# Attention's weight sum replaced by accumulating DMAs, conversions moved to slots 7 to 16, the feed-forward's weight tiles allocated by name, and its first gate tile loaded in unit 26

## The chip, the cores and the metric

The kernel runs on one core of a Trainium2 chip. The metric is the device time of one execution in microseconds, as the median of several runs. TensorE (PE) multiplies, VectorE (DVE) and ScalarE (ACT) do elementwise work, GpSimd (POOL) too, and SyncE (SP), POOL and ACT issue DMAs. TensorE's granted clock is 1.2 or 2.4 GHz; in the tables 1.00 is the higher of them and 0.50 the lower.

## The reference

Three stages follow each other. Sizes: 4 batches, 8 heads, 576 tokens a batch, head size 64, model width 512, 8 experts of width 1024, a feed-forward layer of width 2048, 2304 tokens in all.

```
phi(x):  proj = x @ w_phi;  proj -= max|proj| over the row
         [exp(proj), exp(-proj)]
attention: kv = phi(k)^T @ v;  z = sum of phi(k)
           x = (phi(q) @ kv) / (phi(q) @ z + 1e-6)
experts:   e = argmax of the token's cosine logits / tau, gate = its softmax
           x = gate * (relu(x @ w1[e]) @ w2[e])
layer:     h = x @ w_in;  out = (h * sigmoid(h)) @ w_out
```

The weights w_in and w_out arrive in 64 bits and are converted on the chip.

## The kernel before

**Attention** runs over 32 heads, one iteration of a loop each. PE projects a head three iterations ahead; DVE takes the row maximum of the projection and subtracts it (`shift`, lines 385 and 386), which frees the projection's place in PSUM for the next head; PE multiplies the numerators and denominators of the current one (`numden`, line 474). ACT takes exponentials, and POOL the low parts of values that are split into a high and a low float for exact products.

**Conversion.** w_in and w_out are cut into 16 tiles each, w_in by columns and w_out by rows. `narrow` turns 128x512 numbers of 64 bits into 32 bits in four steps (one multiplication, on DVE in attention and on ACT later, then lines 201 or 204, 206 and 208 on DVE). Two neighbouring tiles of w_in make one weight `q` of the eight (NJP); its products use a scheme with seven combinations of four 128x256 blocks a0, a1 (of the even tile, with turned sign) and b0, b1 (of the odd one), kept in DRAM as `sscr[q]` with seven places. The even tile goes to places 0 and 1. For an odd tile `narrow` has a fifth step, the weight sum b0 + b1 (line 214), and `keep_weights` stores b0 in place 6, b1 in 2 and the sum in 3, 4 and 5. `add_weights(q, 0)` then adds place 0 to places 4, 5 and 6 with one accumulating DMA on POOL's queue, and `add_weights(q, 1)` adds place 1 to place 5. The first ten tiles (CA) are converted in attention, through the generator `Convert.step`, a few steps an iteration; the fifth step of an odd tile is the last before the next iteration's `shift`. Tiles 10 to 15 are converted in the expert stage.

**Experts.** 22 slots of 128 tokens. In slot s PE multiplies x by w1 in four parts (`mm1`), then the relu'd product of the slot before by w2 in four parts (`mm2`); it turns inputs with `xturn` (line 858) and hidden values with `hturn`. ACT and DVE split the weights (`split`, lines 837 and 838); SP loads them (`load1`, `load2`, line 801), only where the expert changes. POOL issues the gathers of tokens two slots ahead (`gather`, line 823), one add of `add_weights` a slot (slots 1 to 14, 17 and 18), and for the conversions a load (`cload`) and a store (`cstore`). A list `HOOKS` of places in slots gives the conversions five steps each: the first four call `cwork`, the first of which also loads the tile after next, and the fifth stores. Raw data has two buffers and the result one (`J[i]`).

**Layer.** 32 units, 8 for each of four blocks of 576 tokens: unit u multiplies weight q = u mod 8 in seven products `prod(u, n)`, in the order n = 1, 5, 4 of the unit before, 6, 3 of the unit before, 2, 7. ACT copies (`keep`, line 1083) and DVE joins (`join`, line 1090) the results; SP stores them to `hd` (line 1096). A written plan `at(unit, n, task)` hangs tasks behind products: the conversion of w_out (`oload`, `cwork`, `cstore`), and from unit 26 on `ofetch`, `ohigh`, `olow`, which load eight converted output weights of 512 KB and split them (lines 1124, 1127, 1131). The gate tile `gload(i)` reads 128 tokens of `hd` (1 MB, line 1143) and `gate` applies the activation, the high cast and the low subtraction (lines 1157 to 1159); `down` multiplies by the output weights. `gload(0)` takes a buffer of the pool `ul` that the conversions of w_out used before; `gload(1)`, `gload(2)` and later ones take buffers of pool `dr`, which is opened, on the right side of the memory, when `ur` with the tiles `wb` of weights 4 to 7 is closed. All engines' orders are as written, and DMAs of one queue are issued in that order. A tile of a later pool waits for the readers of the tiles on whose place it lies (`reuse_waits="tile"`).

```
htile(0, (0, 0))
for q in (4, 7, 6, 5):
    wspace(q)
wfetch(4)
wfetch(5)
```

Of the kernel before, what the change touches and what calls it, by code (L numbers as in the profile page):

```python
# [10 lines left out]
F32R = mybir.dt.float32r  # L11
# [3 lines left out]
ALU = mybir.AluOpType  # L15
# [4 lines left out]
P = 128  # L20
# [12 lines left out]
NJ = FF2 // P  # L33
TN = 288
NJP = NJ // 2
# [9 lines left out]
CA = 10  # L45
# [21 lines left out]
def moe_kernel(ctx, tc, qk, v, w_phi, emb, tau, w1, w2, win, wout, out):  # L67
    nc = tc.nc
# [10 lines left out]
    sscr = [dram.tile([P, 7, 256], F32, name=f"sscr{i}") for i in range(NJP)]  # L79
# [91 lines left out]
    def keep_weights(i, c, rw, dma=nc.sync):  # L171
        half, j = divmod(i, NJ)
        q, odd = divmod(j, 2)
        c = c.bitcast(F32)
        if half:
            dma.dma_start(out=woscr[q][:, odd, :], in_=c)
        elif odd:
            both = rw.rearrange("p f t -> p (f t)")[:, 0:256].bitcast(F32)
            dma.dma_start(out=sscr[q][:, 6, :], in_=c[:, 0:256])
            dma.dma_start(out=sscr[q][:, 2, :], in_=c[:, 256:512])  # L180
            dma.dma_start(out=sscr[q][:, 3:6, :], in_=both.unsqueeze(1).to_broadcast([P, 3, 256]))
        else:
            dma.dma_start(out=sscr[q][:, 0:2, :], in_=c.rearrange("p (a f) -> p a f", a=2))

    def add_weights(q, n):
        src = sscr[q][:, n:n + 1, :]
        if n:
            nc.gpsimd.dma_start(out=sscr[q][:, 5:6, :], in_=src, accum_op=ALU.add)
        else:
            nc.gpsimd.dma_start(out=sscr[q][:, 4:7, :], in_=src.to_broadcast([P, 3, 256]), accum_op=ALU.add)  # L190

    def narrow(rw, c, eng, i):
        minus = i < NJ and i % 2 == 0
        lo, hi = rw[:, :, 0], rw[:, :, 1]
        if eng is nc.scalar:
            nc.scalar.mul(out=c.bitcast(F32), in_=hi.bitcast(F32), mul=2.0 ** -112)
        else:
            eng.tensor_scalar(out=c.bitcast(F32), in0=hi.bitcast(F32), scalar1=2.0 ** -112, scalar2=None, op0=ALU.mult)
        yield
        if minus:  # L200
            nc.vector.tensor_scalar(out=lo, in0=lo, scalar1=29, scalar2=-2147483648, op0=ALU.logical_shift_right,
                                    op1=ALU.bitwise_or)
        else:
            nc.vector.tensor_scalar(out=lo, in0=lo, scalar1=29, scalar2=None, op0=ALU.logical_shift_right)
        yield
        nc.vector.scalar_tensor_tensor(out=c, in0=c, scalar=3, in1=lo, op0=ALU.logical_shift_left, op1=ALU.bitwise_or)
        yield
        nc.vector.scalar_tensor_tensor(out=c, in0=hi, scalar=-2147483648, in1=c, op0=ALU.bitwise_and,
                                       op1=ALU.bitwise_xor)
        if i < NJ and i % 2:  # L210
            yield
            a, b = c.bitcast(F32)[:, 0:256], c.bitcast(F32)[:, 256:512]
            both = rw.rearrange("p f t -> p (f t)")[:, 0:256].bitcast(F32)
            nc.vector.tensor_tensor(out=both, in0=a, in1=b, op=ALU.add)
# [32 lines left out]
    def phase_all(ctx):  # L247
# [517 lines left out]
        pools = {}  # L765
# [48 lines left out]
        def load2(s, parts=(0, 1)):  # L814
            if s < 2:
                st["e", s] = (nc.sync.value_load(regs_a[0:1, 2, POS[s]:POS[s] + 1], min_val=0, max_val=E - 1), None)
            fetch(raw2, w2, s, parts)

        def gather(s):
            xg = mp.tile([P, DM], F32, tag="t2a", name="xg", bufs=3)  # L820
            n = (B - 1) * S if s < NP else NT
            p = POS[s]
            nc.gpsimd.indirect_dma_start(out=xg, out_offset=None, in_=xd[0:n, :],
                                         in_offset=bass.IndirectOffsetOnAxis(ap=gidx[:, p:p + 1], axis=0))
            st["xg", s] = xg
# [116 lines left out]
            next(todo, None)  # L942
            keep_weights(i, c, rw, dma)

        HOOKS = [(s, n) for s in (2, 3, *range(7, 17)) for n in ((1, 5, 7) if s % 2 == 0 and s > 2 or s == 3 else (1, 5))]

        def convert(s, n):
            if (s, n) not in HOOKS:
                return
            i, n = divmod(HOOKS.index((s, n)), 5)  # L950
            if n == 0 and i and CA + i + 1 < NJ:
                cload(CA + i + 1)
            if n < 4:
                cwork(CA + i)
            else:
                cstore(CA + i, nc.gpsimd)
# [7 lines left out]

        def wspace(q):
            wb = (big.tile([P, 2, 2048], F32R, tag="blk", name="wb") if q < 4 else
                  pools["ur"].tile([P, 2, 7 * 256], F32R, tag="wb", name="wbr", bufs=4))
            W[q] = (wb[:, 0, 0:7 * 256], wb[:, 1, 0:7 * 256])

        def wfetch(q):  # L970
            if q < 4:
                wspace(q)
            nc.sync.dma_start(out=W[q][1].bitcast(F32), in_=sscr[q].rearrange("p a f -> p (a f)"))
# [77 lines left out]
        def xsplit(k, name):  # L1051
            xhigh(k, name)
            xlow(k, name)
# [215 lines left out]
        for g in range(-2, G):  # L1269
            b, h = divmod(g, H)  # L1270
# [133 lines left out]
        def route(*key):  # L1404
            if key in PLAN:
                next(more)
# [7 lines left out]
        for s in range(1, NSF + 1):  # L1414
            if s + 1 < NSF:
                load2(s + 1, (0,))
            if 1 < s < NSF:
                load2(s, (1,))
            if s == 20:
                wfetch(0)  # L1420
            if s == 21:
                wfetch(1)
                wfetch(2)
            if s < NSF:
                if s + 2 < NSF:
                    gather(s + 2)
                q, n = divmod(s - 1 if s < 15 else s - 3 if s > 16 else 99, 2)
                if q < NJP:
                    add_weights(q, n)
                for k in range(4):  # L1430
                    mm1(s, k)
                    if (s, k) == RANK:
                        ranks(B - 1, rbank)
                    route(1, s, k)
                    if s + 1 < NSF and k < 3:
                        split(s + 1, 1, k)
                    convert(s, k)
                    if k > 1 and 18 <= s < 21 and 2 * (s - 18) + k - 2 < 5:
                        xscale(0, 2 * (s - 18) + k - 2)
                    if s == NSF - 1:  # L1440
                        for f, *a in TAIL[k]:
                            f(*a)
                relu(s)
                if s + 1 < NSF:
                    xturn(s + 1)
                    split(s + 1, 1, 3)
            if 1 < s:
                ystore(s - 2)
            if s == 17:
                rp_ctx.close()  # L1450
                x_ctx.close()
                bm_ctx.close()
                sp = ctx.enter_context(tc.tile_pool(name="sp", bufs=2, **T))
                xfetch(0, 0)
                xfetch(0, 1)
            for i in range(4):
                mm2(s - 1, i)
                if s < NSF:
                    split(s, 2, i)
                else:  # L1460
                    for f, *a in TAIL[4 + i]:
                        f(*a)
                route(2, s - 1, i)
                if i == 0 and s + 3 < NSF:
                    load1(s + 3, (0,))
                if i == 0 and s + 2 < NSF:
                    load1(s + 2, (1,))
                convert(s, 4 + i)
                if i > 1 and 18 <= s < 21:
                    n = 2 * (s - 18) + i - 2  # L1470
                    if n < 5:
                        xprep(0, n)
                        if n < 3:
                            xfetch(0, n + 2)
                    else:
                        xsplit(0, "B11")
            if s < NSF:
                hturn(s)
            if s == NSF - 1:
                xfetch(1, 0)  # L1480
                xfetch(1, 1)
                wfetch(3)
            if s < NSF:
                yout(s - 1)
            if s == NSF - 1:
                for n in (1, 5, 2):
                    prod(0, n)
# [11 lines left out]
        def at(u, n, *task):  # L1499
            todo.setdefault((u, n), []).append(task)  # L1500

        htile(0, (0, 0))
        for q in (4, 7, 6, 5):
            wspace(q)
        wfetch(4)
        wfetch(5)
        def plan():
# [33 lines left out]
                at(27 + m, 6, ohigh, 2 * m + 1)  # L1541
                at(27 + m, 3, olow, 2 * m + 1)
            at(24, 7, nc.scalar.activation, vec[0:1, 0, 0:1], vec[0:1, 0, 0:1], AF.Silu)
            at(29, 1, gload, 0)
            at(30, 6, gate, 0, 0)
            at(31, 6, gate, 0, 1)

# [27 lines left out]
    with ExitStack() as c2:  # L1575
        phase_all(c2)
# [31 lines left out]
```

## Time and profile before

| | |
|---|---|
| median of three runs | 939.63 us (939.2 to 941.2) |
| the profiled execution | 941.78 us, of which the span of the trace is 940.1 us |
| busy in the span | PE 909.0, DVE 629.5, ACT 583.6, POOL 253.1 us |
| mean granted clock of PE | 0.989 |

Attention takes about the first 240 us, the experts lie up to about 530, the layer's units up to 731 and its second product up to the end. A busy engine is one that has an instruction under way; the ends of PE's instructions are modelled. Times are counted from the span's start. In rows of the timeline the first number is the start and the second the duration, or the whole stretch where several instructions are merged (x4), and the bracket holds the idle time before it and what ended it.

### The profile page before, as it was taken

To read this page: it belongs to the slowest core of one execution; us is meant where nothing else is said; L and a number is where in the kernel's file an instruction comes from. 1 tells how busy PE (TensorE), PEld (TensorE's weight loads), DVE (VectorE), ACT (ScalarE), POOL (GpSimd) and SP (SyncE) were. 2 spreads that over 40 slices of the span, in tenths; PEclk is the share of its full clock that TensorE was granted. 3 is DMA by queue.
4 is the path that set the end of the run, shared out by engine and by line. 5 is a ranking of instruction groups with operands and counts; after the bars stand their busy time and mean duration, and the time that the engine had idled before them with its cause. 6 is when DMAs were issued, how large, how long until landed. Compare 5 with 4: busy or idle time off the path is not lost. (4 is left out here: it accounts for less than half of the span.)

```text
span 940.1 us, 15670 instructions
## 1 busy us (share of the span) xinstructions
PE 909.0 (97%) x5567; PEld 791.5 (84%) x5567; DVE 629.5 (67%) x976; ACT 583.6 (62%) x948; POOL 253.1 (27%) x231
## 2 busy tenths in 40 slices
PE   8999999999999999999999899999997899999997
PEld 6999999988777778888888799999997688888885
DVE  7889898986799989989988756575763122222221
ACT  6777878745977778889888664444453233444441
POOL 6878877712212503222200020201000100010000
PEclk9999999999999999999999999999998899999999
DMA  6455353349486825993697565877694844444420
GB/s 179 115 143 171 91 177 92 102 138 355 169 218 208 257 101 177 323 305 116 218 374 267 201 202 175 253 241 244 227 311 128 202 112 112 113 112 118 118 68 22
DMA packets 135106, 170.50 MB, mean 181 GB/s; under 512 B 34696, under 2 KB 95880, under 8 KB 135024
## 3 DMA queue, kind: packets, MB, share of 16 engines
q1 hardware_dynamic: 124432, 144.84, 49.0%
q0 software_dynamic: 10512, 24.58, 9.3%
q8 instruction: 45, 0.74, 0.3%
q14 instruction: 37, 0.30, 0.1%
q10 hardware_dynamic: 80, 0.03, 0.0%
HBM read 169.43 MB, written 50.33 MB: 234 GB/s over the span
## 5 line engine op out<-in xcount | busy, mean ns | idle before, releaser
L838 DVE TENSOR_TENSOR wl<-raw,wh 128x1024 fp32r<-128x1024 f32 (+1 forms) x166 | 189.1, 1178 | 26.8 <-ACT wh L837 21.0
L837 ACT CAST wh<-raw 128x1024 fp32r<-128x1024 f32 (+1 forms) x166 | 161.4, 1025 | 24.1 <-DMA raw<-w 10.7
L1159 DVE TENSOR_TENSOR hlt<-gt,hlt 128x1024 fp32r<-128x1024 f32 x34 | 41.7, 1226 | 153.3 <-ACT hlt L1158 153.3
L788 PE MATMUL po<-wob,hlt 128*128 128x512 f32 x272 | 107.8, 396 | 3.9 <-ACT hlt L1158 3.9
L1083 ACT COPY ht<-puA 128x288 f32<-128x288 f32 x128 | 50.8, 399 | 96.4 <-PE puA L790 82.1
L790 PE MATMUL po<-wob,hlt 128*128 128x512 f32 x272 | 109.6, 403 | 0.0
L789 PE MATMUL po<-wob,hlt 128*128 128x512 f32 x272 | 108.2, 398 | 0.0
L424 POOL TENSOR_TENSOR kl<-ke,kh 128x640 fp32r<-128x640 f32 x52 | 85.2, 1657 | 31.9 <-issue 23.6
L1179 ACT COPY os<-po 128x512 f32<-128x512 f32 x17 | 10.0, 586 | 107.7 <-PE po L790 107.7
L474 PE MATMUL pnx<-kv,qp 128*128 128x73 f32 x640 | 76.6, 275 | 0.0
L474 PEld LDWEIGHTS pnx<-kv,qp 128*128 128x128 f32 x640 | 74.1, 192 | 0.1
L1180 POOL DMA_INDIRECT out<-os,oidx x18 | 17.9, 994 | 185.7 <-ACT os L1179 175.2
L788 PE MATMUL ph<-wh,xh 128*128 128x512 f32 x166 | 67.1, 404 | 0.0
L790 PE MATMUL ph<-wh,xl 128*128 128x512 f32 x166 | 65.3, 393 | 1.0 <-DVE xl L845 1.0
L788 PEld LDWEIGHTS po<-wob,hlt 128*128 128x128 f32 x272 | 51.8, 190 | 16.4 <-ACT hlt L1158 4.3
L789 PE MATMUL ph<-wl,xh 128*128 128x512 f32 x166 | 64.8, 390 | 0.0
L789 PEld LDWEIGHTS po<-wob,hlt 128*128 128x128 f32 x272 | 51.7, 190 | 13.5
L790 PEld LDWEIGHTS po<-wob,hlt 128*128 128x128 f32 x272 | 51.6, 190 | 12.6 <-DVE hlt L1159 0.8
L409 ACT ACTIVATE ke<-d 128x640 f32<-128x640 f32 x52 | 38.3, 737 | 38.1 <-DVE d L386 38.1
L385 DVE TENSOR_REDUCE m<-pqk 128x10 f32<-128x1280 f32 x32 | 47.6, 1486 | 19.1 <-PE pqk L379 19.1
L1090 DVE TENSOR_TENSOR ht<-puC,ht 128x288 f32<-128x288 f32 x64 | 29.1, 454 | 46.7 <-PE puC L790 41.8
L379 PE MATMUL pqk<-wbd,zh 128*128 128x256 f32 (+1 forms) x320 | 59.5, 285 | 0.8 <-DVE d L386 0.6
(405 smaller groups left out, 2445.8 us busy)
## 6 DMA issues: line engine op xcount, KB each, us to landing
raw<-w SPq DMA_DIRECT2D x44, 1536.0 KB
raw<-w SPq DMA_DIRECT2D x44, 512.0 KB
hd<-ht SPq DMA_DIRECT2D x124, 144.0 KB
gt<-hd SPq DMA_DIRECT2D x15, 1024.0 KB
z<-qk SPq DMA_DIRECT2D x32, 288.0 KB
wo<-wout SPq DMA_DIRECT2D x17, 512.0 KB
yd<-ys SPq DMA_DIRECT2D x23, 256.0 KB
raw<-win SPq DMA_DIRECT2D x10, 512.0 KB
```

Of the source, the lines that this page charges most:

```text
L379: nc.tensor.matmul(out=pqk[0:r, c * 256:(c + 1) * 256], lhsT=z[:, c * P:c * P + r], rhs=wbd[:, j].rearrange("p h f -> p (h f)"), start=(i ...
L385: nc.vector.tensor_reduce(out=m, in_=pv, axis=AX.X, op=ALU.max, apply_absolute_value=True)
L409: nc.scalar.activation(out=ke, in_=kd, func=AF.Exp, scale=1.0 - 2.0 * s)
L424: nc.gpsimd.tensor_tensor(out=kl[:, :, s, :], in0=st.pop(("ke", g, s)), in1=kh[:, :, s, :].bitcast(F32), op=ALU.subtract)
L474: nc.tensor.matmul(out=pn[:, c, 0:73], lhsT=qp[:, s, c * P:(c + 1) * P], rhs=kv[:, s, 0:73], start=(s == 0), stop=(s == 1))
L788: nc.tensor.matmul(out=o, lhsT=ah, rhs=bh, start=first, stop=False, skip_group_check=more)
L789: nc.tensor.matmul(out=o, lhsT=ah, rhs=bl, start=False, stop=False, skip_group_check=more)
L790: nc.tensor.matmul(out=o, lhsT=al, rhs=bh, start=False, stop=last, skip_group_check=more)
L837: nc.scalar.copy(out=hi[:, 0:n], in_=sl[:, 0:n])
L838: nc.vector.tensor_tensor(out=lo[:, 0:n], in0=sl[:, 0:n], in1=hi[:, 0:n].bitcast(F32), op=ALU.subtract)
L1083: nc.scalar.copy(out=htile(u, at), in_=BK[u, "A"])
L1159: nc.vector.tensor_tensor(out=lo, in0=g, in1=hi.bitcast(F32), op=ALU.subtract)
```

## The change

The fifth step of `narrow` is left out for tiles in attention. Their odd tiles store b0 in place 6 and b1 in places 2 to 5, and a third add, (q, 6), later adds place 6 to places 3, 4 and 5. The adds of weights 0 to 4 are thus three, those of 5 to 7 two; the list `ADDS` has 21, and slot s issues two of them from slot 8 on. `HOOKS` begins in slot 7 and has three places in each slot to 16. The tiles of weights 4 to 7 get a tag each and are allocated in rising order. `gload(0)` is called behind `prod` 4 in unit 26 instead of behind `prod` 1 in unit 29.

```diff
--- before.py
+++ after.py
@@ -174,6 +174,9 @@
         c = c.bitcast(F32)
         if half:
             dma.dma_start(out=woscr[q][:, odd, :], in_=c)
+        elif i < CA and odd:
+            dma.dma_start(out=sscr[q][:, 6, :], in_=c[:, 0:256])
+            dma.dma_start(out=sscr[q][:, 2:6, :], in_=c[:, 256:512].unsqueeze(1).to_broadcast([P, 4, 256]))
         elif odd:
             both = rw.rearrange("p f t -> p (f t)")[:, 0:256].bitcast(F32)
             dma.dma_start(out=sscr[q][:, 6, :], in_=c[:, 0:256])
@@ -182,12 +185,13 @@
         else:
             dma.dma_start(out=sscr[q][:, 0:2, :], in_=c.rearrange("p (a f) -> p a f", a=2))
 
+    ADDS = [(q, n) for q in range(NJP) for n in ((6, 0, 1) if 2 * q < CA else (0, 1))]
+
     def add_weights(q, n):
+        a, b = {6: (3, 6), 0: (4, 7), 1: (5, 6)}[n]
         src = sscr[q][:, n:n + 1, :]
-        if n:
-            nc.gpsimd.dma_start(out=sscr[q][:, 5:6, :], in_=src, accum_op=ALU.add)
-        else:
-            nc.gpsimd.dma_start(out=sscr[q][:, 4:7, :], in_=src.to_broadcast([P, 3, 256]), accum_op=ALU.add)
+        nc.gpsimd.dma_start(out=sscr[q][:, a:b, :], in_=src.to_broadcast([P, b - a, 256]) if b - a > 1 else src,
+                            accum_op=ALU.add)
 
     def narrow(rw, c, eng, i):
         minus = i < NJ and i % 2 == 0
@@ -207,7 +211,7 @@
         yield
         nc.vector.scalar_tensor_tensor(out=c, in0=hi, scalar=-2147483648, in1=c, op0=ALU.bitwise_and,
                                        op1=ALU.bitwise_xor)
-        if i < NJ and i % 2:
+        if CA <= i < NJ and i % 2:
             yield
             a, b = c.bitcast(F32)[:, 0:256], c.bitcast(F32)[:, 256:512]
             both = rw.rearrange("p f t -> p (f t)")[:, 0:256].bitcast(F32)
@@ -942,7 +946,7 @@
             next(todo, None)
             keep_weights(i, c, rw, dma)
 
-        HOOKS = [(s, n) for s in (2, 3, *range(7, 17)) for n in ((1, 5, 7) if s % 2 == 0 and s > 2 or s == 3 else (1, 5))]
+        HOOKS = [(s, n) for s in range(7, 17) for n in (1, 5, 7)]
 
         def convert(s, n):
             if (s, n) not in HOOKS:
@@ -964,7 +968,7 @@
 
         def wspace(q):
             wb = (big.tile([P, 2, 2048], F32R, tag="blk", name="wb") if q < 4 else
-                  pools["ur"].tile([P, 2, 7 * 256], F32R, tag="wb", name="wbr", bufs=4))
+                  pools["ur"].tile([P, 2, 7 * 256], F32R, tag=f"wb{q}", name="wbr", bufs=1))
             W[q] = (wb[:, 0, 0:7 * 256], wb[:, 1, 0:7 * 256])
 
         def wfetch(q):
@@ -1424,8 +1428,7 @@
             if s < NSF:
                 if s + 2 < NSF:
                     gather(s + 2)
-                q, n = divmod(s - 1 if s < 15 else s - 3 if s > 16 else 99, 2)
-                if q < NJP:
+                for q, n in ADDS[max(2 * s - 16, 0):max(2 * s - 14, 0)]:
                     add_weights(q, n)
                 for k in range(4):
                     mm1(s, k)
@@ -1500,7 +1503,7 @@
             todo.setdefault((u, n), []).append(task)
 
         htile(0, (0, 0))
-        for q in (4, 7, 6, 5):
+        for q in range(4, NJP):
             wspace(q)
         wfetch(4)
         wfetch(5)
@@ -1541,7 +1544,7 @@
                 at(27 + m, 6, ohigh, 2 * m + 1)
                 at(27 + m, 3, olow, 2 * m + 1)
             at(24, 7, nc.scalar.activation, vec[0:1, 0, 0:1], vec[0:1, 0, 0:1], AF.Silu)
-            at(29, 1, gload, 0)
+            at(26, 4, gload, 0)
             at(30, 6, gate, 0, 0)
             at(31, 6, gate, 0, 1)
```

## Rows read from the trace of the kernel before

**Rows 1.** Busy time, granted clock (PEclk), DMA share and rate of five stretches, one answer

```profile
336.30:339.90 3.60, 3.60 (x11) 2.78 (x10) 2.97 (x4) 3.60 (x6) 0.00 (x0) 0.54 0.39 146
360.00:425.00 65.00, 65.00 (x312) 52.59 (x311) 60.72 (x73) 56.80 (x82) 21.63 (x22) 1.00 0.92 301
683.00:712.00 29.00, 27.60 (x209) 27.37 (x207) 15.80 (x25) 14.22 (x27) 0.00 (x0) 1.00 0.97 308
716.60:722.10 5.50, 5.46 (x23) 5.47 (x24) 1.85 (x3) 1.14 (x3) 0.00 (x0) 0.50 0.32 109
740.50:746.00 5.50, 5.40 (x12) 3.82 (x13) 3.36 (x3) 4.50 (x6) 1.38 (x1) 0.50 1.04 265
```

**Rows 2.** PE in order of time, where it waited

```profile
334.97 0.50 PE L788 MATMUL py<-wh,hh 128*128 128x512 f32 x1 [1.97 <-ACT hh L842]
...
716.64 0.61 PE L788 MATMUL puC<-xcT1n,wbr 128*128 128x288 f32 x1 [6.04 <-DVE ht L1090]
...
736.29 0.39 PE L790 MATMUL po<-wob,hl 128*128 128x512 f32 x1
740.56 0.79 PE L788 MATMUL po<-wob,hlt 128*128 128x512 f32 x1 [3.89 <-ACT hlt L1158]
```

**Rows 3.** PE in order of time, the numerators of three heads

```profile
38.40 2.40 PE L474 MATMUL pnx<-kv,qp 128*128 128x73 f32 x20
...
45.11 2.40 PE L474 MATMUL pnx<-kv,qp 128*128 128x73 f32 x20
...
52.72 1.50 PE L474 MATMUL pnx<-kv,qp 128*128 128x73 f32 x12
```

**Rows 4.** DVE in order of time, the weight sum of one tile

```profile
45.10 1.65 DVE L214 TENSOR_TENSOR raw<-raw 128x256 f32<-128x256 f32 x1
```

**Rows 5.** One line: its count, duration in ns (min/median/max), first and last start

```profile
L214 DVE TENSOR_TENSOR raw<-raw x5: 416/1653/1658, 45.1 to 196.9; 128x256 f32<-128x256 f32 x5
```

**Rows 6.** POOL in order of time, an add and a conversion's load

```profile
317.15 1.36 POOL L190 DMA_DIRECT2D sscr<-sscr  x1
317.99 1.35 POOL L169 DMA_DIRECT2D x<-win  x1
```

**Rows 7.** ACT in order of time, the expert stage

```profile
333.82 0.62 ACT L837 CAST wh<-raw 128x512 fp32r<-128x512 f32 x1 [8.05 <-DMA raw<-w]
```

**Rows 8.** SP's queue in order of time, units 26 to the end

```profile
685.72 0.49 SPq L1124 DMA_DIRECT2D wob<-woscr  x1
...
700.55 0.45 SPq L1143 DMA_DIRECT2D g<-hd  x1
701.09 5.92 SPq L1096 DMA_DIRECT2D hd<-ht  x2
707.07 0.45 SPq L1124 DMA_DIRECT2D wob<-woscr  x1
707.61 18.16 SPq L1096 DMA_DIRECT2D hd<-ht  x9
731.27 27.84 SPq L1143 DMA_DIRECT2D gt<-hd  x6
```

**Rows 9.** ACT in order of time, units 27 to the end

```profile
691.11 1.05 ACT L1127 CAST wob<-wob 128x1024 fp32r<-128x1024 f32 x1
...
711.88 1.04 ACT L1127 CAST wob<-wob 128x1024 fp32r<-128x1024 f32 x1 [3.67 <-DMA wob<-woscr]
...
738.38 1.06 ACT L1157 ACTIVATE gt<-gt 128x1024 f32<-128x1024 f32 x1 [7.50 <-DMA gt<-hd]
```

**Rows 10.** What SP's queue waited for: us in total, times, longest

```profile
SPq L1143 <- PE puC L790: 5.4, 1, 5.4
```

**Rows 11.** DMAs by form: count, size, median us to landing

```profile
sscr<-sscr POOLq DMA_DIRECT2D x8, 384.0 KB, 9.2
```

**Rows 12.** PE in order of time, the input turns of two slots

```profile
374.56 0.60 PE L858 MATMUL pxt<-ident,xg 128*128 128x128 f32 x4
...
386.99 0.60 PE L858 MATMUL pxt<-ident,xg 128*128 128x128 f32 x4
```

## What I expect, and why

> **What bounds the kernel now.** I read the busy time by stretch first: TensorE (PE) is busy nearly throughout [rows 1]. So an edit counts only where it fills a hole in PE's work, or lengthens a stretch that PE waits for. I then read whom PE waits for [rows 2]: three waits stand out, 6.0 us behind a join on VectorE (DVE), 3.89 us behind a cast on ScalarE (ACT), 1.97 us behind another. Each is followed by a stretch in which the granted clock is 0.50 or little more, the lower of the two levels, 1.2 instead of 2.4 GHz [rows 1]; PE's work takes twice as long there. The two late ones are 5.5 us long and cost half of that, 2.75 each; the early one is 3.6 us long and costs 1.8. So the three holes are worth 6.0 + 2.75 = 8.8, 3.9 + 2.75 = 6.6 and 2.0 + 1.8 = 3.8 us. A fourth loss shows only in the rhythm of attention: PE starts the numerators of successive heads 6.71 us apart, but 7.61 us apart where the weight sum stands on DVE between them [rows 3, 4].
>
> **The change part by part.** *No weight sum.* Five sums of 128x256 leave DVE in attention; median 1.653, longest 1.658 and shortest 0.416 us, so at least three are long [rows 5], and I take four. DVE is late by such a sum when it reaches the next head's maximum. The head after the sum at 45.10 takes 7.61 instead of 6.71, so each long sum costs PE 0.90; the short one I put at nothing. Four are 3.6 us (ends: 0, if another wait takes the place; 4.5, if the fifth costs as much). The stores keep their bytes: 128 KB and four copies of 128 KB, in two DMAs instead of three on SP's queue, which hides under attention.
>
> *Adds and conversions leave slots 1 to 7.* The 2.0 us hole ends at 334.97 [rows 2]. ACT there stood 8.05 us for an expert weight [rows 7]. In the same stretch POOL issued a 384 KB add at 317.15 and a 512 KB conversion load at 317.99 [rows 6], and a small add around each. Afterwards these are gone. But POOL runs ahead of the slots, since nothing in slots 2 to 7 but the gathers holds it, so the first new add, also 384 KB, can still start early, by my estimate near 322. One large transfer of two stays. The weight need come only 2.0 us earlier for PE not to wait, and at the stretch's rate, some 300 GB/s (301 in a full stretch [rows 1]), 512 KB less are 1.7 us. I take 3.0 of the 3.8 (ends 0 and 3.8).
>
> *The same adds, and five more, in slots 8 to 18.* Slots are 12.43 us [rows 12]. Slots 8 to 15 now hold fifteen adds of weights 0 to 4 instead of seven in all, and each weight's three depend on each other, so POOL, which issues in order, stands until the one before has landed: 9.2 us at the median for 384 KB [rows 11]. Behind it queue the gathers, needed over a slot later, the conversion's load, and its store. The store matters: the next conversion writes the same staging buffer, now often two hooks later, and its first instruction is on ACT. Ten waits of 9.2 and fifteen issues of some 1.2 (an estimate from the 1.36 us of the add at 317.15 [rows 6], the small ones being shorter) are 110 us against 8 x 12.43 = 99. Weight 0's first two lie ahead of slot 8, so 8 x 9.2 + 18 = 92, and it just fits. What ACT can lose unseen is read from the hole in slot 6: 8.05 idle became 1.97 of PE, so 6 us are cover. I expect ACT to stand some 5 us at the stores of the fourth and fifth conversion, about at that edge, and also weights in 360 to 425, where the DMA queues are already at 0.92 [rows 1], to land later. I take +3 us (ends 0 and +10).
>
> The Trainium skill, page "DMA: Bandwidth & Descriptors", section "Anatomy of one DMA — SWDGE (gpsimd) path", prices such a DMA at about 2.0 us plus its bytes by 436 GB/s. That would be an estimated 2.9 us for 384 KB; the rows say 9.2. By the page POOL would never be late and the term would be 0.
>
> *First gate tile in unit 26.* It is now issued at 700.55, as a transfer of 1 MB. The next DMA on SP's queue, a small one whose data was long there, then took until 707.0 for two issues (5.92 us), and so the last output weight was issued at 707.07 [rows 8]. ACT got it at 711.88, after 3.67 us of standing [rows 9], and behind its cast lie the gate's activation and cast, DVE's subtraction and then the join that PE waits for: PE resumes at 716.64, 4.7 us later [rows 2]. Moved to unit 26, the load keeps its price but blocks the second output weight instead, issued now at 685.72 [rows 8]. It must also wait until the store of the previous conversion has read its buffer. I put the gate load at about 688, the weight's issue at 690 and its landing at 694.5 (1.5 MB at some 300 GB/s are 5 us, and what is queued goes ahead). ACT wants it at 691.11 [rows 9]. It stands 3.4 us; PE has about 1.7 us of cover there, so some 1.7 lost. In unit 30 the last weight is then on time, but the 4.7 us chain remains on ACT and DVE, and PE reaches that join 3.2 us after its own last product before the weight (four products of 0.8), with 0.5 for ACT's copy: 2.0 us idle, perhaps 1.8 of half clock as in slot 6. Together 5.5 to 5.8 instead of 8.8: I take -3.0 (ends -6.9, no stall but the 2.0 idle, and +5, if two waits of ACT are added where the queues are at 0.97 [rows 1]).
>
> *Weight tiles by name.* SP's next gate load stood 5.4 us for a product of PE [rows 10], was issued at 731.27 and ACT waited for it until 738.38, 7.50 us [rows 8, 9]. The pools explain it. Both end at the same edge: `ur` has 11 h tiles of 1,152 bytes, four weights of 14,336 and 9,216 behind; `dr` has six of 8,192. So the first gate buffer lies 30,080 bytes into `ur`, which is in the second weight. With the order 4, 7, 6, 5 that is weight 7, read by the very last products; by name in rising order it is weight 5, done two units earlier. The third and fourth places hold 6 and 7, so the second load waits for weight 6 at most. The load then goes at about 725.8, right behind SP's last tile stores (18.16 us from 707.61 [rows 8]), and lands 7 us later at 733; activation and cast take 2.1, the subtraction 1.2; PE has work until 736.5 [rows 2]. The hole closes: -6.6 (ends 0 and -6.6). At the start of the stage the fetch of weight 5 may wait for a later reader, but its cast comes three units later, which covers it.
>
> **Sum.** -3.6 - 3.0 + 3.0 - 3.0 - 6.6 = -13.2. The profiled execution took 941.78 (span 940.1 and 1.7 around it), so 928.6 on its scale; it lies 2.15 above the median of the three timed runs, 939.63. On the median: 926.4.
>
> **The rivals.** (a) *The gate tiles still wait*, because the pool places the named tiles otherwise. For it: the trace shows no addresses. Against: the wait for the last product fits the sizes exactly. 926.4 + 6.6 = 933.0.
> (b) *The early gate load costs as much as before or more.* For it: the queues at 0.97, eight weights just in time. +5 instead of -3: 934.4.
> (c) *The adds starve the expert weights* (slower). Slots 8 to 15 gain about eight large adds; each reads and writes 384 KB, 6.3 MB in all, at 301 GB/s 21 us; the stretch 360 to 425 has 8% or 5 us free. If all fall into it, 16 us, and twice 2.7 us of half clock after stalls: 926.4 - 3 + 21.4 = 944.8. It decides from about 18 us of lost PE time, so nearly all eight must fall there. I count four, and POOL's own waits spread them. Against it too: part of the weights' lateness is covered by ACT's 6 us.
> (d) *The adds cost nothing*, as landings are short in the calm stretches and POOL's lateness stays under cover: 923.4. The page named above would have it so; the rows speak for some 9 us each.
> (e) *Nothing moves*: the holes are filled by new waits of the same length (a late gather, ACT behind a store): 939.6.
>
> **How the numbers follow.** Forecast 0.54, (a) 0.10, (b) 0.12, (c) 0.08, (d) 0.10, (e) 0.06. A difference under 0.2% (1.9 us) is about what a measurement can't tell from none. Faster: 0.54 + 0.10 + 0.12 + 0.10 = 0.86; same 0.06; slower 0.08. The best ends together (-3.6 - 3.8 + 0 - 6.9 - 6.6) give 918.7; the forecast's own range is 919 to 932. For 8 in 10 I take 918.5 to 936, which takes in (a), (b) and (d).
>
> **What would show it.** Right: the heads after DVE's third and fourth conversion step 6.71 apart throughout; no 8 us ACT wait near 334; the first `gt` load issued right behind SP's last `hd` store, no PE wait on `hlt`; the long SP issue now in unit 26, with an ACT wait on `wob` there, and a shorter PE wait on a join in unit 30. Wrong: POOL waiting for its own adds while ACT's first conversion step or a `pxt` transpose waits; the wait of `gt` on `puC` still there; or a PE wait above 6 us in units 27 to 31.

## The result, and the profile after

The changed kernel takes 944.70 us at the median (942.84 to 946.56, 7 runs) beside 939.63; the ratio is 1.0058, 95% interval 1.0038 to 1.0078. It is slower by half a per cent, where I expected 926.4.

Both traces have 5,567 instructions on PE in the same order. The start of the n-th in one less that in the other shows stage by stage where time went. In us, after less before, with the time of before at which a stage ends; the last column is the sum of the others:

| attention, first slots (to 317) | slots 6 and 7 (to 346) | slots 8 to 20 (to 505) | to unit 26 (690) | gate tile (to 730) | second product begins (755) | all, at PE's last instruction |
|---|---|---|---|---|---|---|
| -3.6 | -4.3 | +17.6 | -0.5 | -0.7 | -6.9 | +1.7 |

All five terms of the sum have the sign expected, but the third is six times its size and the fourth a quarter of it. The span is 2.9 longer, 1.2 of it behind PE's last instruction; the rest of the 5.1 between the medians is that the profiled execution of before lies 2.15 above its median, that of after (943.0 + 1.7) at it.

PE of the kernel after in order of time, where it waited:

```profile
384.52 0.80 PE L792 MATMUL py<-wh,hh 128*128 128x512 f32 x1 [4.85 <-ACT hh L846]
...
386.53 0.80 PE L794 MATMUL py<-wh,hl 128*128 128x512 f32 x1 [0.80 <-DVE hl L849]
...
410.37 1.97 PE L894 MATMUL ht<-ident,hs 128*128 128x128 f32 x8 [3.30 <-ACT hs L882]
...
706.87 0.61 PE L792 MATMUL puA<-xcT,wb 128*128 128x288 f32 x1 [2.86 <-ACT ht L1087]
...
727.77 0.40 PE L792 MATMUL puC<-xcT1n,wbr 128*128 128x288 f32 x1 [1.98 <-DVE ht L1094]
...
745.13 0.39 PE L792 MATMUL po<-wob,hlt 128*128 128x512 f32 x1
```

The three waits of [rows 2] are gone or shorter: none at the place of the one of 1.97 us, 1.98 in place of 6.04 at the join, none at 745.13, where it was 3.89. The one of 1.97 is what the prediction calls the hole of slot 6; counted by the order of PE's work it lies in the second half of slot 7, where the hidden values of slot 6 are multiplied, and it is called the hole at 335 here. New waits stand in slots 11 and 12 and in unit 27. Busy time and clock by stretch, columns as in [rows 1]:

```profile
345.00:490.00 145.00, 134.92 (x624) 106.84 (x622) 118.47 (x139) 108.90 (x158) 59.55 (x46) 0.94 0.83 230
384.50:390.50 6.00, 5.19 (x11) 3.68 (x12) 6.00 (x9) 6.00 (x10) 2.51 (x2) 0.50 0.88 284
412.00:416.00 4.00, 4.00 (x12) 3.13 (x11) 3.74 (x5) 4.00 (x7) 1.23 (x2) 0.50 1.12 313
707.00:713.00 6.00, 6.00 (x25) 6.00 (x26) 4.14 (x6) 2.81 (x5) 0.00 (x0) 0.50 0.97 315
727.70:733.00 5.30, 5.23 (x38) 5.19 (x39) 1.95 (x5) 2.91 (x5) 0.00 (x0) 1.00 0.33 111
```

Behind each new wait PE runs at 1.2 GHz again; behind the 1.98 us at 727.77 it does not. What ended the idle time is read from ACT in order of time:

```profile
381.87 0.66 ACT L200 ACTIVATE x<-x 128x512 f32<-128x512 f32 x1 [10.79 <-DMA sscr<-x]
...
408.23 0.66 ACT L200 ACTIVATE x<-x 128x512 f32<-128x512 f32 x1 [8.88 <-DMA sscr<-x]
...
705.47 1.04 ACT L1131 CAST wob<-wob 128x1024 fp32r<-128x1024 f32 x1 [4.97 <-DMA wob<-woscr]
...
742.04 1.06 ACT L1161 ACTIVATE gt<-gt 128x1024 f32<-128x1024 f32 x1 [2.56 <-DMA gt<-hd]
```

The first two are the first steps of conversions, which wait until the stores of the conversion before have read the one staging buffer. At the first of them that data was ready on DVE at 364.73; the sum, which lies in another buffer, at 368.41:

```profile
364.06 0.67 DVE L212 SCALAR_TENSOR_TENSOR x<-x 128x512 int32<-128x512 int32 x1
...
368.00 0.41 DVE L218 TENSOR_TENSOR x<-x 128x256 f32<-128x256 f32 x1
```

On POOL in order of time two adds stand ahead of its three stores, the second waiting for the first:

```profile
362.41 1.30 POOL L193 DMA_DIRECT2D sscr<-sscr  x1 [5.13 <-DMA sscr<-sscr]
370.63 0.85 POOL L193 DMA_DIRECT2D sscr<-sscr  x1 [6.92 <-DMA sscr<-sscr]
371.19 0.88 POOL L182 DMA_DIRECT2D sscr<-x  x1
371.81 0.81 POOL L183 DMA_DIRECT2D sscr<-x  x1
372.37 1.00 POOL L184 DMA_DIRECT2D sscr<-x  x1
```

The two stores that read the staging buffer are thus issued 6.5 us after their data was ready, at 371.19 and 371.81, when ACT already stands (from 371.08), and then they take long. The time from issue to landing of the DMAs to `sscr`, first in before for three such stores (407.3 to 409.9), then in after for the add at 370.63 with its three stores:

```profile
DMA to landing us min/median/max: 2.8/3.0/7.4
```

```profile
DMA to landing us min/median/max: 9.6/9.9/10.4
```

The add, of 128 KB, and the stores behind it all land some 10 us after their issue. Of the three in before the two that read the staging buffer take 2.8 and 3.0, that of the sum 7.4. ACT goes on at 381.87, when the store issued at 371.81 has landed.

### The profile page after: what moved, and what is told of

It is laid out like the page before. It is cut to its first block, busy times and chain, and to the rows that moved or that the text cites. A ratio compares the mean times of both kernels' runs of the same rounds, so it can differ in the third digit from the quotient of the medians.

```text
span 943.0 us, 15659 instructions
## 1 busy us (share of the span) xinstructions
PE 909.5 (96%) x5567; PEld 793.2 (84%) x5567; DVE 619.6 (66%) x971; ACT 580.9 (62%) x948; POOL 270.1 (29%) x236
## 5 line engine op out<-in xcount | busy, mean ns | idle before, releaser
L793 PE MATMUL po<-wob,hlt 128*128 128x512 f32 x272 | 108.5, 399 | 0.0
L792 PE MATMUL po<-wob,hlt 128*128 128x512 f32 x272 | 107.2, 394 | 0.0
L794 PE MATMUL po<-wob,hlt 128*128 128x512 f32 x272 | 106.6, 392 | 0.0
L794 PEld LDWEIGHTS po<-wob,hlt 128*128 128x128 f32 x272 | 51.1, 188 | 12.5 <-DVE hlt L1163 0.2
```

Of the source, the lines that this page charges most:

```text
L792: nc.tensor.matmul(out=o, lhsT=ah, rhs=bh, start=first, stop=False, skip_group_check=more)
L793: nc.tensor.matmul(out=o, lhsT=ah, rhs=bl, start=False, stop=False, skip_group_check=more)
L794: nc.tensor.matmul(out=o, lhsT=al, rhs=bh, start=False, stop=last, skip_group_check=more)
```

## The experiments

All times are medians in us, with the ratio to the kernel before on the same chip; before took 937.45 to 939.63 there, so a difference between two runs of the table can be off by some 2 us. The stage columns are those of the table above, from the one profiled execution of each; executions of one kernel spread by up to 11 us where the slots stall.

| run | median | ratio (95%) | 317 | 346 | 505 | 690 | 730 | 755 |
|---|---|---|---|---|---|---|---|---|
| after | 944.70 | 1.0058 (1.0038 to 1.0078) | -3.6 | -4.3 | +17.6 | -0.5 | -0.7 | -6.9 |
| two_bufs | 937.96 | 0.9987 (0.9972 to 1.0002) | -4.0 | -4.3 | +10.5 | -1.3 | -1.2 | -6.9 |
| adds_spread | 937.41 | 0.9980 (0.9969 to 0.9991) | -3.9 | -4.3 | +12.4 | -0.7 | -1.6 | -6.9 |
| no_adds | 927.07 | 0.9898 (0.9870 to 0.9926) | -3.9 | -4.3 | -0.2 | -1.4 | -2.4 | -6.9 |
| hooks_old | 940.08 | 1.0013 (0.9988 to 1.0038) | -2.7 | -2.9 | +14.0 | -0.7 | -2.5 | -6.9 |
| store_act | 931.40 | 0.9920 (0.9896 to 0.9943) | -3.9 | -4.3 | +10.6 | +0.8 | -2.2 | -6.9 |
| adds_last | 939.13 | 1.0012 (0.9998 to 1.0026) | -4.1 | -4.3 | +12.5 | +1.8 | -2.6 | -6.9 |
| gate29 | 945.01 | 1.0060 (1.0041 to 1.0080) | -3.7 | -4.3 | +19.5 | -0.4 | -1.4 | -6.9 |
| gate26_only | 937.65 | 0.9988 (0.9976 to 1.0000) | +0.3 | -2.9 | +0.9 | -1.1 | +0.3 | 0.0 |
| gate_halves | 940.89 | 1.0011 (0.9992 to 1.0031) | -3.7 | -4.3 | +16.9 | -0.9 | -5.8 | -6.9 |
| tags_only | 930.92 | 0.9910 (0.9891 to 0.9928) | +0.1 | -2.1 | +1.0 | +0.1 | +0.1 | -6.9 |
| fix_a | 928.75 | 0.9905 (0.9889 to 0.9921) | -4.0 | -4.3 | +4.5 | +0.4 | -3.6 | -6.9 |
| fix_b | 927.75 | 0.9894 (0.9878 to 0.9910) | +0.2 | -1.9 | +0.5 | -0.4 | -6.6 | -6.9 |
| fix_c | 925.63 | 0.9873 (0.9857 to 0.9890) | -4.0 | -4.3 | +5.1 | -0.7 | -8.0 | -6.9 |
| fix_d | 924.89 | 0.9868 (0.9847 to 0.9888) | -3.2 | -2.5 | +0.5 | -1.1 | -7.9 | -6.9 |
| fix_e | 924.12 | 0.9848 (0.9829 to 0.9866) | 0.0 | -2.5 | +1.6 | -1.1 | -8.7 | -6.9 |

**What the adds cost.** Without them (no_adds):

```diff
                 for q, n in ADDS[max(2 * s - 16, 0):max(2 * s - 14, 0)]:
-                    add_weights(q, n)
+                    pass
```

> The changed kernel without its 21 accumulating adds; the weights of the combinations stay unsummed, so the output is another one. Theory A (the adds alone, by the stores, the gathers and the weights that they delay): all of the 17 us between slots 7 and 18 goes: about 928 (926 to 930). Rival C (the denser conversion steps take part of it): 932 to 940.

927.07, 17.6 less than after, within 1 us of theory A. PE has no hole left in the slots, with the conversions as dense as before, so rival C falls:

```profile
345.00:490.00 145.00, 145.00 (x715) 117.24 (x714) 134.24 (x156) 126.89 (x184) 31.68 (x27) 1.00 0.69 244
```

**Through what.** A second buffer for the converted data (two_bufs) leaves every queue as it is:

```diff
-                    scr[:, 2048:2560].bitcast(I32)]
+                    (scr[:, 2048:2560] if i % 2 else c2).bitcast(I32)]
...
+        c2 = rp.tile([P, 512], F32, name="c2")
         cload(CA)
```

> The changed kernel with a second staging buffer for the results of the conversions in the expert stage; same traffic, same order of every queue. Theory A (the stores stand on POOL's queue behind the accumulating adds, and ACT's next first conversion step waits for the one buffer that they read): ACT's waits of 10.8 and 8.9 us for the store are gone, PE's two holes of 4.8 and 3.3 us with the half clock behind them too, some 15 to 16 us: about 929 (926 to 932). Rival B (the adds' traffic is what takes the time, whatever waits for it): other waits of the same size take their place, above all ACT waiting for expert weights; 940 or more.

ACT's waits for stores are gone, and up to 410 us of before PE is level with no_adds and 16 us ahead of after, as A says. But 937.96 is 6.7 less and not 16: two other waits then end later, for a gather that POOL issues behind its adds, and for a copy that ACT makes late, having stood 4.38 us for an expert weight.

```profile
PE pxt L862 <- DMA xg<-xd,gidx: 3.9, 1, 3.9
...
PE pt L1013 <- ACT xf L1019: 3.5, 1, 3.5
```

Rival B is thus half right: the stores were the first wait to end last, not the only one.

Why does a store take 10 us: for the add ahead of it on POOL's queue, or for full engines? The stores on ACT's queue (store_act):

```diff
-                cstore(CA + i, nc.gpsimd)
+                cstore(CA + i, nc.scalar)
```

> The changed kernel with the conversions' stores in the expert stage issued on ACT's queue instead of POOL's; adds, traffic and the one staging buffer as they are. Theory D (a store of 128 to 256 KB takes 8 to 10 us to land because it stands behind an add on POOL's queue): the stores land in 2 to 4 us as before, ACT's waits for the buffer are gone, and the time is that of the second buffer, 938. Rival E (the store is slow because the 16 DMA engines are full in this stretch, on whichever queue): waits of 8 to 10 us stay, 944.

931.40, below the 938 that D gave. ACT's waits for stores, in total, times and longest, first after, then here:

```profile
ACT x L200 <- DMA sscr<-x: 22.3, 3, 10.8
```

```profile
ACT x L200 <- DMA sscr<-x: 3.3, 2, 2.8
```

And the engines are no emptier here, 0.99 for 360 to 425 where after has 0.92:

```profile
360.00:425.00 65.00, 62.32 (x291) 49.07 (x290) 53.76 (x63) 48.82 (x73) 19.21 (x16) 1.00 0.99 313
```

So the waits came from the place on POOL's queue, where the stores go late and land late, and E falls as their cause. It keeps a share: the store of 256 KB issued on ACT's queue at 388.94 let ACT go on only at 395.80, 6.9 us later, with no add ahead of it. And not every store behind an add takes 10 us. In adds_spread, below, the add of 128 KB at 443.62 landed in 3.5 us and the store behind it in 3.6, and in after those at 421.68 in 7.4 and 6.3 to 6.6. In all of these the stores landed just after the add, 0.2 to 2.6 us later; why the add itself takes 3.5 us or 9.6 stays open.

The Trainium skill, page "DMA: Bandwidth & Descriptors", section "Two DMAs through the same engine are not ordered", says that within one queue of one DMA engine descriptors start in order but overlap; stores that land right behind the add agree. Its section "Issuing engines are not separate DMA queues", by which another issuing engine saves only the time on the sequencer, does not agree with the fall of ACT's waits from 22.3 to 3.3 us. The 13.3 us between the medians are less sure: the profiled execution of this run is the slowest of its four, 4.1 above the median, and still loses 10.6 in the slots, 6 of them near 480, where ACT stood 3.63 us for an expert weight.

The same adds at the end of a slot (adds_last; the two lines of the loop are moved ahead of `hturn(s)`):

> The changed kernel with the same two adds a slot, issued at the slot's end instead of its start. The store of the second conversion (behind product 1 of slot 10) then still follows adds on POOL's queue, that of the third (behind product 7 of slot 11) has a slot's time since the last ones. Theory D: the first wait of some 10 us stays, with its hole of 4 to 5, the second goes: about 938 to 940. Rival E (full engines): both stay, 944.

939.13, the number that D gave, by luck, for it was not made as D said. The first wait shrank to 1.6 us, the second to 5.6: both adds of slot 9 were issued at 359.8 before the data was ready, while the second add of slot 10 ran late ahead of the second store. The loss moved to the gathers, behind which PE stood twice:

```profile
PE pxt L862 <- DMA xg<-xd,gidx: 6.5, 2, 4.0
```

**Where the adds stand.** One a slot in slots 1 to 13, two a slot in 14 to 17 (adds_spread):

```diff
-                for q, n in ADDS[max(2 * s - 16, 0):max(2 * s - 14, 0)]:
+                for q, n in ADDS[s - 1:s] if s < 14 else ADDS[2 * s - 15:2 * s - 13]:
```

> The changed kernel with its 21 adds spread: one a slot in slots 1 to 13, two a slot in 14 to 17. Theory A (stores behind adds): in slots 10 and 11 a store has one add ahead of it instead of two in a chain, so ACT's waits shrink from 10.8 and 8.9 to about 4, inside its cover of 6, and the holes go: -14; the slot 6 hole may come back for up to +4: 931 to 935. Rival B (traffic): eight adds fewer in slots 8 to 13 give about half of the 17 us back: 936, with the rest of the waits on expert weights. Rival C (three conversion steps a slot are what is too dense): 944 or so, as the steps are unchanged.

937.41, above A and nearest to B's 936. Both holes go, as A says, and with them 16 us by slot 13; then an expert weight comes 6.5 us late at 405.8, and a store behind the two adds of slot 15 holds ACT for 9.3 at 447.8. The hole at 335 did not come back.

The late adds with the conversions' old places (hooks_old; `HOOKS` of the kernel before):

> The changed kernel with the conversions' places of the kernel before (slots 2, 3, 7 to 16), and the new adds. Theory A: a store stands at the end of an even slot, the next first step some 3 us later, while the second of the slot's two adds is issued some 9 us after the slot's start; so ACT waits as long as before or longer, 20 us and more in sum, and the hole of slot 6 comes back with 4: 945 to 950. Rival C (density of the conversion steps): 935 or less.

940.08, 4.6 less than after instead of the same or more, and above C's 935: ACT waits 17.9 us for stores, but for two of them. With the adds two a slot the stage loses under either set of places, 14.0 us here and 17.6 in after. Beside adds_spread this run tells what closes the hole at 335: with the adds back in the early slots and the conversions moved it is closed (-4.3), with the adds late and the conversions in their old places a wait of 0.5 us stays there (-2.9). It is the conversions' move, not that of the adds.

**The gate tile.** Back in unit 29 (gate29; `at(29, 1, gload, 0)`), and alone in the kernel before (gate26_only; `at(26, 4, gload, 0)`):

> The changed kernel with the first gate tile's load back behind product 1 of unit 29. Theory from the two traces (the load in unit 26 costs 2.9 us of hole and 2.75 of half clock in unit 27 and 2.0 in unit 30, against 6.0 and 2.75 in unit 30): +0.8, about 945.5. The step as predicted (moving the load is worth 3.0): 947.7. Rival (the load in unit 26 lies where the queues are fullest and costs more than it gives once the rest is changed): 942.

> The kernel before with only the first gate tile's load moved to unit 26. Theory from the changed kernel's trace: a hole of 2.9 us and 2.75 of half clock in unit 27 and 2.0 of hole in unit 30, against 8.8 before; -0.8, so 938.8. The step as predicted: 936.6. Rival (without the conversions' shift the queues stand otherwise and the load costs more): 942.

945.01 beside 944.70, and 937.65 beside 938.25 for before on the same chip: moving this load changes nothing that is clear of the spread. PE of gate26_only, where it waited:

```profile
694.38 0.40 PE L788 MATMUL puA<-xcT,wb 128*128 128x288 f32 x1 [2.42 <-ACT ht L1083]
...
714.07 0.61 PE L788 MATMUL puC<-xcT1n,wbr 128*128 128x288 f32 x1 [3.43 <-DVE ht L1090]
```

One hole of 6.04 has become two of 5.85 together. Two halves of 512 KB instead (gate_halves; `js` is eight of the sixteen rows of tiles):

```diff
+            if half is not None:
+                js = slice(8 * half, 8 * half + 8)
+                nc.sync.dma_start(out=t[:, js, :], in_=hd[0][js, :, 0:P].rearrange("j p t -> p j t"))
+                return
...
-            at(26, 4, gload, 0)
+            at(28, 3, gload, 0, 0)
+            at(30, 1, gload, 0, 1)
```

> The changed kernel with the first gate tile loaded in two halves of 512 KB, one in unit 28 and one in unit 30, in place of 1 MB in unit 26. Theory (what costs is that a load of 1 MB holds SP's next issues back while the eight output weights are due one after the other): the hole and half clock of unit 27 go, 5.7 us, the 2.0 of unit 30 stays at most: 937 to 939. Rival (any further 512 KB among the output weights makes one of them late): a hole of 2 to 4 us with half clock in units 28 to 30: 942 to 946.

940.89, 3.8 less than after; the trace gives 5.1 in this stage, near the theory's 5.7, and the median lies between its 937 to 939 and the rival's 942. SP's queue: the next store follows the first half within 1.6 us and the second within 0.5, where the whole tile took 5.92 for two stores [rows 8].

```profile
706.41 0.42 SPq L1149 DMA_DIRECT2D g<-hd  x1
708.03 0.32 SPq L1100 DMA_DIRECT2D hd<-ht  x1
...
713.70 0.44 SPq L1149 DMA_DIRECT2D g<-hd  x1
714.22 14.31 SPq L1100 DMA_DIRECT2D hd<-ht  x7
```

**The weight tiles alone** (tags_only; the two lines of the diff that name them and order them):

> The kernel before with only the weight tiles by name in rising order. Theory (the second weight's place is where the first gate buffer of the last stage lies; by name it holds weight 5, done two units earlier): the wait of 7.5 us for the gate tile and its hole of 3.9 us with 2.75 of half clock are gone: 933.0. Rival (the load still waits for another reader, of the third and fourth place): half or nothing of it, 936 to 939.6.

930.92, and -6.9 at the place. Names and order were changed together; no run parts them. SP issues the load at 725.31, straight behind its last store, and ACT waits 2.40 instead of 7.50:

```profile
725.31 26.13 SPq L1143 DMA_DIRECT2D gt<-hd  x6
```

```profile
732.52 1.06 ACT L1157 ACTIVATE gt<-gt 128x1024 f32<-128x1024 f32 x1 [2.40 <-DMA gt<-hd]
```

**Together.** fix_a is after with the second buffer, the adds spread and the halves; fix_c adds one line to it; fix_d is fix_c with one buffer and the old places of the conversions; fix_b is before with the names and the halves; fix_e is fix_b with the same line:

```diff
-            at(30, 6, gate, 0, 0)
+            at(30, 2, gate, 0, 0)
```

> The changed kernel with the second staging buffer, the adds spread one a slot and the first gate tile in two halves. Theory (the stage's loss is the sum of what the adds hold up: stores, 16 us, then gathers and weights): below the 927 of the kernel without adds minus the 5 of the halves, 922, plus the hole of some 5 us behind the expert weight near 405 that the spread adds showed: 926 to 928. Rival (each fix only hands the loss to the next waiter): 932 or more.

> The kernel before with the weight tiles by name and the first gate tile in two halves alone; weight sum, adds and conversions as before. Theory: 930.9 with the names alone; of the 8.8 us in unit 30 a hole of 2.0 to 2.8 stays and the half clock goes: 925. Rival (the halves gain only in the changed kernel, where all else in the stage is later): 930.

> As the first of this group (second buffer, adds spread, halves), with the first half's activation, cast and subtraction behind product 2 instead of 6 of unit 30, that is behind the joins that PE waits for. Theory: the last hole there, 2.0 to 2.8 us, goes: 2 to 2.5 less than the first. Rival (ACT's activation then delays the copy that the next unit needs): no change.

> The changed kernel with the adds spread, the halves and the late activation, but with one staging buffer and the conversions' places of the kernel before. Theory (the move of the conversions is what closes the hole of slot 6, and a store right before the next conversion's first step stalls ACT): about 4 us for slot 6 and some 4 for stores above the third of this group. Rival (the places don't matter once the adds are spread): the same time.

> The kernel before with weight tiles by name, the first gate tile in two halves and the late activation; weight sum, adds and conversions as before. Beside the fastest kernel so far (924.9, which has no weight sum and five more adds, one a slot) it tells what the first part of the change is worth once its adds are spread. Theory (the 3.6 of attention are kept): 924.9 + 3.6 = 928.5 at most, less where the extra adds cost something. Rival (the extra adds give it all back): 924 to 925.

fix_a: 928.75, just above its 926 to 928. The hole behind the expert weight near 405 is there (ACT stands 7.38 us), as counted; what falls short are the halves, -3.6 instead of -5.8, with a hole of 3.3 us at the join. fix_b: 927.75, 3.2 less than the names alone and not 6, although its trace shows the theory's -6.6, with a hole of 2.0 us left at the join. The profiled execution of tags_only is the slowest of its four, 3.2 above their median; what the others lose in this stage no trace shows. The late activation takes the rest of the hole: fix_c is 3.1 below fix_a and fix_e 3.6 below fix_b. fix_d refutes its theory: 924.89 is no slower than fix_c, though 1.8 of the hole at 335 come back. With one add a slot, one buffer and the old places no store holds ACT for over 2.3 us, the 21 adds cost PE 0.3 us between 345 and 490, and the weight near 405 is in time:

```profile
345.00:490.00 145.00, 144.71 (x711) 116.71 (x710) 134.47 (x154) 125.64 (x182) 43.11 (x38) 1.00 0.82 258
```

fix_e, without any of the first and second part of the change, reaches 924.12, the same within the intervals. So what the sum left out gains in attention (3.2 in fix_d's trace) is not there at the end in the median; fix_d's executions lie between 921.6 and 926.6, and its profiled one is the fastest of them. Which wait takes the rest back in the others stays open. Of the four parts of the change only the names of the weight tiles are shown to lower the median by themselves.

## Why the prediction was wrong

*The weight sum* was right. PE starts the numerators of successive heads 6.71 apart where the sum stood [rows 3]. Set start by start beside before, PE gains 0.9 at each of the four long sums (45, 73, 121 and 169 us) and nothing at the short one: 3.6, as the term says. That the table has -3.6 at 317 too is partly luck: 0.5 lost elsewhere in attention and 0.6 gained behind 310 offset each other.

```profile
38.66 2.40 PE L478 MATMUL pnx<-kv,qp 128*128 128x73 f32 x20
45.37 2.40 PE L478 MATMUL pnx<-kv,qp 128*128 128x73 f32 x20
52.08 2.17 PE L478 MATMUL pnx<-kv,qp 128*128 128x73 f32 x18
```

*The hole at 335* closed: -4.3 where I took -3.0. But four kernels that have the code of before up to there show 1.9 to 2.9 less at this place than the profiled execution (tags_only, gate26_only, fix_b, fix_e): a hole of 0.5 to 1.5 us, without half clock. So about 2.3 of the 4.3 were that execution's own. I took its 2.15 above the median off the whole sum and yet counted the hole in full; on the median's scale the term is some -2.0.

*The same adds, and five more, in slots 8 to 18* is the step that failed: +17.6 instead of +3, beyond its end of +10. The mechanism was named, ACT standing at a store behind POOL's adds, and the 6 us of cover held: waits of 10.8 and 8.9 became holes of 4.85 and 3.30, with 0.8 more behind the first, and the half clock behind each. Wrong was the size of the wait, 5 us, put at the edge of the cover. The sum counts how late POOL gets to the store and has no term for how late the store then lands. By late issue alone ACT would have stood some 3.5 us at the first one, an estimate: the store goes at 371.81, lands 2.8 later as in before, and ACT is there from 371.08. It landed after 10.0, behind the add, and that made 10.8. The sign that the prediction gave first for being wrong came true, POOL waiting for its own adds while ACT's first conversion step waits. The sum for POOL as a whole was even too high, eight to ten waits of 9.2, where it was 58.2 us in 11 and the median add of 384 KB landed in 7.1:

```profile
POOL sscr L193 <- DMA sscr<-sscr: 58.2, 11, 10.4
```

It was the right row [rows 11] in the wrong sum: what follows an add on the queue pays its landing too. The stores hit were those of the stage's second and third conversion, not the fourth and fifth. And behind these waits stood others, gathers and an expert weight, that took back 9 of the 16 us when the stores were relieved.

Rival (c), 944.8, gave the measured time by another cause. Its expert weights did not hold PE in after: between 345 and 505 ACT waited 6.3 us for them where before has 2.7, never over 4.2 at once, inside its cover. A late weight or a late gather cost PE several us at once only where the stores were relieved (two_bufs, adds_spread, adds_last). Rival (d) fell: an add of 384 KB landed in 7.1 us at the median, before in 9.2, and all of them cost 17.6. The estimate of 2.9 us by the Trainium skill, page "DMA: Bandwidth & Descriptors", section "Anatomy of one DMA — SWDGE (gpsimd) path", does not agree with these rows.

*The first gate tile* was worth -0.7 and not -3.0. The last weight was in time, and the join's hole was 1.98 where I worked out 2.0. The price in unit 27 was mis-sized: ACT stood 4.97 us at the second weight and not 3.4, PE lost 2.86 and not 1.7, and PE then ran at half clock from 707 to 713, which I had put behind the other hole: +5.9 in the trace instead of +1.7. SP's queue shows the order that I had expected:

```profile
692.94 0.40 SPq L1128 DMA_DIRECT2D wob<-woscr  x1
...
696.97 0.38 SPq L1147 DMA_DIRECT2D g<-hd  x1
697.40 2.02 SPq L1128 DMA_DIRECT2D wob<-woscr  x1
```

*Weight tiles by name*: -6.9 of -6.6. The load no longer waits, as the addresses worked out from the pools' sizes say; the trace shows no addresses.

The error of 18.3 is, but for rounding, made of 14.6 (adds), 2.3 (gate tile), 2.15 (the profiled execution's own excess), 1.2 behind the last PE instruction, less 1.3 (the hole at 335), 0.3 (tiles) and 0.5 (small drifts).

## What to carry to other kernels

A DMA that waits for the one before it holds up whatever follows on the same queue, first in being issued and then in landing. So ask of each buffer which store frees it and what stands ahead of that store; give such stores another queue, or spread the chain over the time in which the queue has nothing urgent. Relieving the wait that ends last shows the next one: work out how far behind it stands before counting the whole gain. And if a hole is read from one execution that is slower than the median, part of its size may be that execution's.

## What the runs showed of the hardware

Stores of 128 to 384 KB right behind an accumulating DMA on POOL's queue landed just after it: 9.8 to 10.4 us after their issue where the add took 9.6 (after, 370.63), 3.6 where it took 3.5 (adds_spread, 443.62). Three stores in before without one ahead took 2.8, 3.0 and 7.4 us. On ACT's queue, with the engines at 0.99, ACT waited for a store for 2.8 us at most, and one of 256 KB took 6.9 us. The clock fell to 1.2 GHz behind holes of 2.86, 3.30 and 4.85 us; behind 1.98 at 727.77 and, in gate26_only, 2.42 at 694.38 (1.00 for the 5.5 us that follow) it did not, while in before it did behind 1.97 at 334.97 [rows 1, 2]. A hole near 2 us may thus cost itself alone or nearly twice itself. Behind a load of 1 MB in rows of 512 bytes SP's next two issues took 5.92 us in unit 29 of before [rows 8], and the next one 2.02 in unit 26 of after; behind 512 KB the next was done within 2.0.
